# Queueing the query transposition and the copy of the sinks' keys behind the softmax reciprocal

## Chip, core and metric

The kernel runs on one core of a Trainium2 chip. The metric is the device time of one execution in microseconds (us). Three runs of the kernel before took 1175.45, 1173.58 and 1175.04 us; their median is 1175.04 us.

## What is computed

Three stages follow one another. Attention works on 4 batches of 8 heads, 768 positions and 64 channels; each position sees the first `n_sink` = 4 keys and a window of 128 keys. A dense layer with a piecewise activation follows, and then a layer of 8 experts in which each expert takes the 384 tokens that the greedy order of the gate's logits gives it.

```python
scores = scale * np.matmul(q, k.transpose(0, 1, 3, 2))
keep = is_sink | in_window
scores = np.where(keep, scores, -1000000000.0)
scores = scores - np.max(scores, axis=-1, keepdims=True)
a = np.exp(scores)
a = a / (np.sum(a, axis=-1, keepdims=True) + 1e-09)
x = np.matmul(a, v)                      # then (tokens, 512)
h = x @ w_in
g = np.where(h >= 1, h, np.where(h <= -1, 0.0, (h + 1) ** 2 / 4.0))
x = g @ w_out
for e in range(8):                       # tokens by the gate's logits, 384 each
    out[mask] = np.maximum(x[mask] @ w1[e], 0.0) @ w2[e]
```

## The kernel before

The 3072 tokens are cut into 12 blocks of 256, three per batch. Every product of the main path is made of three float32r products of high and low halves, so most tiles come in two parts (`xh` and `xl`, `gh` and `gl`, `sq` and `ql`).

**Attention** of a block runs over four pairs of heads (`attn_steps`; the first two blocks use `attn_steps_f32`, which the change does not touch). In a pair, `load_kq` fetches keys and queries, already cut into blocks of 32, so that one VectorE instruction in `turned` (line 428) transposes them in place. `trans_k` splits the transposed keys into `ks` (ScalarE line 300, VectorE line 301) and copies the 32 sinks' keys beside them (line 306). `trans_q` transposes the queries (line 428 on the tile `qr`) and splits them into `sq` (ScalarE, line 314) and `ql` (VectorE, line 315). `scores` has two matmuls (lines 332 and 333), a VectorE instruction that adds the mask and takes the maximum (335), and the exponential on ScalarE with the sum (337). `norm` of a head adds 1e-9 (342), takes the reciprocal of the two sums (343) and has GpSimd scale the 576 probabilities `pr` of a row in place (351; in the first block of a batch two instructions, 346 and 348). `ptrans` transposes the scaled probabilities on TensorE (370) and splits them into `pt` (372, 373). `pv` multiplies by the values and adds the halves to `xa` (389, 395, 396), and `split` turns `xa` into the layer's input: GpSimd adds (405 or 408), ScalarE makes `xh` (409), GpSimd makes `xl` (410). `split_v` has GpSimd write the values' low half (287).

**The dense layer** (`moe1_steps`) goes over 16 slices of the hidden width per block: `hid` has 12 matmuls (632), two VectorE and two ScalarE instructions (640 to 643), and GpSimd writes `gl` (644); `proj` of the slice two back has 12 matmuls (657). The dense layer of one block runs beside the attention of a later one, and TensorE takes both in one queue.

**The order.** `pipeline` (line 598) strings the steps of the pairs together: while pair `now` goes through `ptrans` and `pv`, the next pair's scores and norms are issued, and then `trans_k` and `trans_q` of the pair two on:

```python
"ptrans0 ptrans1 strans +s00 +s01 +norm0 pv0 +s10 +s11 +norm1 "
"*trans_k *trans_q ^load_kq pv1 +split_v +sinks *load_v split"
```

`Plan` sorts all steps by planned times. A scheduler then puts each engine's instructions into a queue; it may move an instruction ahead of an earlier traced one wherever data allows it. On the chip each engine takes its queue in order. The tiles `ks`, `sq` and `ql` have one buffer each. After the last block's attention the router picks the tokens and the experts run.

Of the kernel before, what the change touches and what calls it, by code (L numbers as in the profile page):

```python
# [1 line left out]

# [5 lines left out]
F32 = mybir.dt.float32  # L8
# [17 lines left out]
P = 128  # L26
NT = S // P
NS = 32
# [46 lines left out]
class Kernel:  # L75
# [174 lines left out]
    def attn_steps(self, blk, xt):  # L250

        nc, a = self.nc, self.a
# [4 lines left out]
        nk = len(kts)  # L257
        for p in range(H // 2):
            st = {}
# [36 lines left out]
            def trans_k(p=p, st=st):  # L296
                ks = st["ks"] = self.at.tile([P, 2, 3, W], F32R, name="ks", tag="ks")
                ps = self.turned(st["k"][:, :4 * nk].rearrange("p n c -> p (n c)")).rearrange("p (t c) -> p t c", c=P)
                for hh, (hs, os) in enumerate(half):
                    nc.scalar.copy(ks[hs, hh, :nk, :P], ps[hs])  # L300
                    nc.vector.tensor_tensor(out=ks[os, hh, :nk, :P], in0=ps[hs], in1=ks[hs, hh, :nk, :P].bitcast(F32),  # L301
                                            op=OP.subtract)
                if first:
                    self.sk[p] = self.kp.tile([P, 2, NS], F32R, name="sk", tag=f"sk{p}")
                    nc.vector.tensor_copy(self.sk[p], ks[:, :, 0, :NS].bitcast(F32))
                nc.vector.tensor_copy(ks[:, :, :nk - 1, P:],
                                      self.sk[p].bitcast(F32).unsqueeze(2).to_broadcast([P, 2, nk - 1, NS]))

            def trans_q(st=st):
                sq = st["sq"] = self.at.tile([P, 2, 2, P], F32R, name="sq", tag="sq")  # L310
                ql = st["ql"] = self.at.tile([P, 2, 2, P], F32R, name="ql", tag="ql")
                x = self.turned(st["q"].rearrange("p h n c -> p (h n c)"))
                flat = lambda t: t.rearrange("p h u q -> p (h u q)")
                nc.scalar.activation(flat(sq), x, AF.Copy, scale=0.125)
                nc.vector.scalar_tensor_tensor(flat(ql), x, 0.125, flat(sq).bitcast(F32), op0=OP.mult, op1=OP.subtract)
# [24 lines left out]
            def norm(hh, st=st):  # L340
                pr, sm = st["pr"][:, :, :, hh], st["sm", hh]
                nc.vector.tensor_scalar(sm[:, 2], sm[:, 1], 1e-9, None, op0=OP.add)
                nc.vector.reciprocal(sm[:, 2], sm[:, 2])  # L343
                r = sm[:, 2]
                if first:
                    nc.gpsimd.tensor_tensor(out=pr[:, 0, W:], in0=pr[:, 0, W:], in1=r[:, 0:1].to_broadcast([P, P]),
                                            op=OP.mult)
                    nc.gpsimd.tensor_tensor(out=pr[:, 1], in0=pr[:, 1], in1=r[:, 1:2].to_broadcast([P, 2 * P + NS]),
                                            op=OP.mult)
                else:  # L350
                    nc.gpsimd.tensor_tensor(out=pr, in0=pr, in1=r.unsqueeze(2).to_broadcast([P, 2, 2 * P + NS]),  # L351
                                            op=OP.mult)
# [67 lines left out]
    def load_blocks(self, t, src, ts):  # L420

        for j in range(2):
            blocks = src[ts[0] * P:(ts[-1] + 1) * P, 32 * j:32 * j + 32].rearrange("(n s) d -> s n d", s=32)
            self.nc.sync.dma_start(t[32 * j:32 * j + 32, :4 * len(ts)], blocks)  # L424

    def turned(self, x):

# [947 lines left out]
@with_exitstack  # L1375
def tile_sink_window_attention__moe__expert_choice(ctx, tc, q, k, v, n_sink, window, w_in, w_out, wg, w1, w2, out):
    a = dict(q=q, k=k, v=v, n_sink=n_sink, window=window, w_in=w_in, w_out=w_out, wg=wg, w1=w1, w2=w2, out=out)
    nc = tc.nc
    K = Kernel(ctx, tc, a)
    K.c = ctx.enter_context(tc.tile_pool(name="const", bufs=1))  # L1380
    dr = ctx.enter_context(tc.tile_pool(name="dr", bufs=1, space=DRAM))
    K.x2d = dr.tile([N, DM], F32, name="x2d")
    xg = dr.tile([B * H * S, D], F32, name="xg")
    K.logits = K.c.tile([P, B * NT, E], F32, name="logits")
    K.sk, K.sv, K.skf, K.svf = {}, {}, {}, {}

    def pipeline(general):
        with ExitStack() as c0:
            c1, c3, c4, cd = (c0.enter_context(ExitStack()) for _ in range(4))
            K.pools(c1.enter_context, c0.enter_context)  # L1390
            K.front_pools(c3.enter_context)
            K.dec = cd.enter_context(tc.tile_pool(name="dec", bufs=2, side="right"))
            if not general:
                K.consts()
            xs = {}
            gw, w_in, w_out, gate_t, gate_m = K.weight_steps()

            def xtiles(b):
                if b not in xs:
                    xs[b] = tuple(K.xp.tile([P, 4, TB], F32R, name=n, tag=n) for n in ("xh", "xl"))  # L1400
                return xs[b]

            def attn(plan, blks, t0, t1):
                if general:
                    for i, b in enumerate(blks):
                        plan.at(t0 + (t1 - t0) * i / len(blks), lambda b=b: K.load_x(b, xg, *xtiles(b)))
                    return
                steps = K.pipeline([p for b in blks for p in (K.attn_steps_f32 if b < NF else K.attn_steps)(b, xtiles)])
                dt = 1 / (len(steps) - 0.5)
                for i, s in enumerate(steps):  # L1410
                    plan.add(t0 + (t1 - t0) * dt * (i - 0.5 * (i > 0)), t0 + (t1 - t0) * dt * (i + 0.5), s)

            K.turn_, K.free = 0, ["U0", "A", "U1", "R", "U2", "A"]
            plan = Plan(tc)
            attn(plan, range(1), 0, T0A)
            attn(plan, range(1, 2), A1, B1)
            plan.at(T0M, lambda: setattr(K, "free", ["A", "A", "R"]))
            x01 = [xtiles(1), xtiles(0)]
            plan.add(T0M, T00, K.moe1_steps(0, lambda: xtiles(0), part=(0, H0)))
            plan.add(T1, T2, K.moe1_steps(1, lambda: xtiles(1)))  # L1420
            plan.add(T2, T3, K.moe1_steps(0, lambda: xtiles(0), part=(H0, FT)))
            plan.at(1, gw)
            if not general:
                plan.at(T0A, K.flags)

            def late():
                cd.close()
                K.late_weights(c1.enter_context)

            for f in range(FT):  # L1430
                t, TD = (D0 + f * DA, DA) if f < H1 else (D1 + (f - H1) * DD, DD)
                plan.at(t if f < H1 else D1 + (f - H1) * DD * WF, lambda f=f: w_in(f))
                if f == FA:
                    plan.at(t + TD / 2, late)
                plan.at(t + TD / 2, lambda f=f: w_out(f))
                plan.at(t + TD / 2 + TG, lambda f=f: gate_t(f))
                plan.at(t + TD / 2 + TG + (TH if f < FA - 1 else 1), lambda f=f: gate_m(f))

            def turn():
                c3.close()  # L1440
                K.router_pools(c0.enter_context)
                hold.append(c4.enter_context(tc.tile_pool(name="hold", bufs=1, side="right")))
                K.router_consts()
                K.rtag = "R"

            def clear():
                c4.close()
                c1.close()
                K.pools2(c0.enter_context)

            hold = []
            b1 = T3 + BLOCK * (NB - 3)
            attn(plan, range(2, 3), TA2, TA3)
            attn(plan, range(3, NB), TA3, b1 - BLOCK * AHEAD)
            for b in range(2, NB - 1):
                plan.add(T3 + BLOCK * (b - 2 - OV), T3 + BLOCK * (b - 1), K.moe1_steps(b, lambda b=b: xtiles(b)))
            plan.at(b1 - BLOCK * OV - 0.5, turn)
            to_logits, rest = K.moe1_steps(NB - 1, lambda: xtiles(NB - 1), lambda: hold[0])
            plan.add(b1 - BLOCK * OV, b1 + HB, to_logits)
            plan.add(b1 + HB, b1 + HB + TP, rest)  # L1460
            plan.at(b1 + HB + TP, clear)
            K.experts(plan, b1 + HB)
            plan.run()

    pipeline(False)
    flag = nc.values_load(K.flag[0:1, 0:1], min_val=0, max_val=1)
    with tc.If(flag):
        with ExitStack() as c0:
            K.attn_general(c0.enter_context, xg)
        pipeline(True)  # L1470
# [32 lines left out]
```

## Time and profile before

| | |
|---|---|
| median of three runs | 1175.04 us |
| time of the profiled execution | 1172.83 us |
| its span (first to last instruction) | 1171.0 us |
| TensorE busy | 1102.2 us, 94% of the span |
| VectorE busy | 872.2 us, 74% |
| ScalarE busy | 698.2 us, 60% |
| GpSimd busy | 487.0 us, 42% |

The profile counts an engine as busy while an instruction of it runs. TensorE is the fullest. Its busy time is modelled from pipelined matmuls, so the rows that matter are those that give the idle time in front of an instruction and the instruction that ended it. In those rows PE is TensorE's matmul, DVE VectorE, ACT ScalarE and POOL GpSimd.

### The profile page before, as it was taken

Reading aid. Unit: us, or ns where it says so; the run is one execution under the profiler, and the core shown is the slowest. Engines: PE = TensorE matmul, PEld = TensorE weight load, DVE = VectorE, ACT = ScalarE, POOL = GpSimd, SP = SyncE. Lnnn points to the kernel's source line nnn. Section 1 sums busy time; section 2 is a strip of 40 time slices with the busy share of each in tenths; the row PEclk is TensorE's granted clock in tenths of the full one; section 3 lists DMA queues with packets and bytes.
Section 4 is the critical chain, followed back from the end, with each engine's and each line's share of the span. In section 5 each row is a group of like instructions: output and inputs, shape, how many; then the busy total and the mean of one; then the engine's idle time right before and its main releaser. Section 6 shows DMA issues by size and latency. Waiting matters only on the chain.

```text
span 1171.0 us, 24367 instructions
## 1 busy us (share of the span) xinstructions
PE 1102.2 (94%) x8256; PEld 1017.4 (87%) x8256; DVE 872.2 (74%) x2718; ACT 698.2 (60%) x1598; POOL 487.0 (42%) x590
## 2 busy tenths in 40 slices
PE   5899888999999999999999999999799999999997
PEld 3688878999999999999999999999587788788896
DVE  5978978777777877776777787755788888788430
ACT  4887777566666666676667676643245445444552
POOL 1335745444545545455545554542213213322321
PEclk9899999999999999999999999999799999999999
DMA  4645522323222222223222222100485767667772
GB/s 105 173 143 158 158 60 61 70 42 64 53 39 56 36 55 49 61 46 64 34 54 49 58 46 56 22 19 1 120 228 168 204 180 216 188 194 202 217 218 66
DMA packets 241928, 118.13 MB, mean 101 GB/s; under 512 B 196096, under 2 KB 220672, under 8 KB 241792
## 3 DMA queue, kind: packets, MB, share of 16 engines
q1 hardware_dynamic: 231504, 85.36, 28.4%
q0 software_dynamic: 8592, 29.89, 10.9%
q8 instruction: 67, 1.10, 0.4%
q10 hardware_dynamic: 1696, 1.22, 0.3%
q14 instruction: 69, 0.57, 0.2%
HBM read 86.00 MB, written 13.11 MB: 85 GB/s over the span
## 4 chain that ended last, share of the span: by engine, by line
PE 42%; DVE 13%; issue 9%; ACT 6%; POOL 5%; DMA 4%; SPq 2%; DVEq 0%; POOLq 0%; ACTq 0%
PE hp L632 11%; PE up L657 11%; PE hp L1048 6%; PE us L1075 6%; PE xp L389 1%; DVE oh L945 1%; ACT pr L337 1%; ACT u L641 1%; PE tp L370 1%; SPq L424 1%; DVE u L640 1%; DVE ind L801 1%; DVE ks L301 1%; DMA qr<-in_q_dram 1%; POOL gl L644 1%
## 5 line engine op out<-in xcount | busy, mean ns | idle before, releaser
L644 POOL TENSOR_TENSOR gl<-u,gh 128x256 fp32r<-128x256 f32 x192 | 149.5, 779 | 205.3 <-ACT gh L643 169.5
L657 PE MATMUL up<-woh,gl 128*128 128x256 f32 x576 | 166.6, 289 | 2.6 <-POOL gl L644 2.6
L657 PE MATMUL up<-woh,gh 128*128 128x256 f32 x576 | 163.7, 284 | 0.0
L657 PE MATMUL up<-wol,gh 128*128 128x256 f32 x576 | 163.5, 284 | 0.0
L641 ACT ACTIVATE u<-u,half 128x256 f32<-128x256 f32 x192 | 97.4, 508 | 83.4 <-DVE u L640 79.4
L632 PE MATMUL hp<-xh,wil 128*128 128x256 f32 x768 | 132.0, 291 | 3.6 <-ACT xh L409 2.8
L632 PE MATMUL hp<-xl,wih 128*128 128x256 f32 x768 | 126.4, 284 | 2.0 <-POOL xl L410 1.6
L632 PE MATMUL hp<-xh,wih 128*128 128x256 f32 x768 | 124.7, 283 | 0.0
L632 PEld LDWEIGHTS hp<-xh,wil 128*128 128x128 f32 x768 | 107.6, 191 | 5.7 <-ACT xh L409 4.2
L657 PEld LDWEIGHTS up<-woh,gl 128*128 128x128 f32 x576 | 108.9, 189 | 3.2 <-POOL gl L644 3.1
L632 PEld LDWEIGHTS hp<-xl,wih 128*128 128x128 f32 x768 | 106.4, 191 | 3.4 <-POOL xl L410 3.4
L657 PEld LDWEIGHTS up<-wol,gh 128*128 128x128 f32 x576 | 108.6, 189 | 0.4 <-issue 0.4
L657 PEld LDWEIGHTS up<-woh,gh 128*128 128x128 f32 x576 | 108.5, 188 | 0.4 <-issue 0.4
L632 PEld LDWEIGHTS hp<-xh,wih 128*128 128x128 f32 x768 | 106.3, 191 | 0.0
L642 DVE TENSOR_TENSOR u<-hp,u 128x256 f32<-128x256 f32 x192 | 80.5, 420 | 31.6 <-ACT u L641 29.8
L640 DVE TENSOR_SCALAR u<-hp 128x256 f32<-128x256 f32 x192 | 79.9, 416 | 31.0 <-PE hp L632 22.5
L351 POOL TENSOR_TENSOR pr<-pr,sm 128x576 f32<-128x576 f32 x56 | 71.3, 1273 | 67.9 <-DVE sm L343 30.3
L643 ACT CAST gh<-u 128x256 fp32r<-128x256 f32 x192 | 77.6, 404 | 30.3 <-DVE u L642 28.0
L337 ACT ACTIVATE pr<-pr,sm 128x288 f32<-128x288 f32 (+1 forms) x160 | 85.2, 533 | 16.3 <-DVE sm L335 15.7
L1056 ACT ACTIVATE hh<-hp 128x384 fp32r<-128x384 f32 x64 | 31.5, 492 | 102.1 <-PE hp L1048 89.4
L373 DVE TENSOR_TENSOR pt<-tp,pt 128x512 fp32r<-128x512 f32 (+1 forms) x80 | 51.3, 647 | 43.9 <-ACT pt L372 43.4
L1075 PE MATMUL us<-w2h,hl 128*128 128x512 f32 x192 | 80.8, 421 | 0.0
(264 smaller groups left out, 3040.0 us busy)
## 6 DMA issues: line engine op xcount, KB each, us to landing
w1r<-in_moe_w_dram SPq DMA_DIRECT2D x32, 512.0 KB, 4.7
w2r<-in_moe_w_dram SPq DMA_DIRECT2D x32, 512.0 KB, 4.5
w2l<-w2r POOLq DMA_DIRECT2D x32, 512.0 KB
qr<-in_q_dram SPq DMA_DIRECT2D x320, 32.0 KB, 1.9
dr<-in_moe_w_in_dram SPq DMA_DIRECT2D x15, 512.0 KB, 4.1
dr<-in_moe_w_out_dram SPq DMA_DIRECT2D x15, 512.0 KB, 3.7
x2d<-ev SPq DMA_DIRECT2D x26, 256.0 KB, 2.2
vr<-in_v_dram SPq DMA_DIRECT2D x56, 96.0 KB, 2.3
```

Source lines behind the costliest of these rows:

```text
L337: nc.scalar.activation(pr, pr, AF.Exp, bias=sm[:, 0, u:u + 1], scale=-1.0, accum_out=sm[:, 1, u:u + 1])
L351: nc.gpsimd.tensor_tensor(out=pr, in0=pr, in1=r.unsqueeze(2).to_broadcast([P, 2, 2 * P + NS]), op=OP.mult)
L373: nc.vector.tensor_tensor(out=pt[:, 1, :n], in0=ps, in1=pt[:, 0, :n].bitcast(F32), op=OP.subtract)
L632: nc.tensor.matmul(ps, w_[:, k, fs], x_[:, k, :], start=(i == 0 and k == 0), stop=(i == 2 and k == 3))
L640: nc.vector.tensor_scalar(u, ps, -1.0, 1.0, op0=OP.max, op1=OP.min)
L641: nc.scalar.activation(u, u, AF.Square, bias=self.half, scale=0.5)
L642: nc.vector.tensor_tensor(out=u, in0=ps, in1=u, op=OP.max)
L643: nc.scalar.copy(gh, u)
L644: nc.gpsimd.tensor_tensor(out=gl, in0=u, in1=gh.bitcast(F32), op=OP.subtract)
L657: nc.tensor.matmul(o, g_[:, ts], self.w_out_part(w_, f)[:, cs], start=(f == fa and i == 0 and (cs.start > 0 or t == 0)), stop=(f == fz - 1 ...
L1048: nc.tensor.matmul(ps, w_[:, k, fs], x_[:, k, :], start=(i == 0 and k == 0), stop=(i == 2 and k == 3))
L1075: nc.tensor.matmul(us[j], h_[:, o], w_[:, f % 2, :], start=(f == 0 and i == 0), stop=(f == nf - 1 and i == 2))
```

## The change

Two VectorE instructions of the preparation of a pair, the sinks' copy (line 306) and the transposition of the queries (line 428 on `qr`), get an ordering edge without a semaphore: the scheduler may not put them ahead of the reciprocal that was traced last. No instruction is added or removed. The transposition of the keys, the split of the keys (line 301) and `ql` carry no edge. The first attention block that goes through `attn_steps` has no reciprocal to stand behind for its first pair; the other 39 pairs do.

```diff
-                nc.vector.tensor_copy(ks[:, :, :nk - 1, P:],
-                                      self.sk[p].bitcast(F32).unsqueeze(2).to_broadcast([P, 2, nk - 1, NS]))
+                with self.behind_shares():
+                    nc.vector.tensor_copy(ks[:, :, :nk - 1, P:],
+                                          self.sk[p].bitcast(F32).unsqueeze(2).to_broadcast([P, 2, nk - 1, NS]))
...
-                x = self.turned(st["q"].rearrange("p h n c -> p (h n c)"))
+                with self.behind_shares():
+                    x = self.turned(st["q"].rearrange("p h n c -> p (h n c)"))
...
-                nc.vector.reciprocal(sm[:, 2], sm[:, 2])
+                self.shares = nc.vector.reciprocal(sm[:, 2], sm[:, 2]).ins
...
+    def behind_shares(self):
+
+        return self.tc.issue_after(self.shares) if self.shares else nullcontext()
```

`issue_after(i)` gives every instruction traced in its block on the engine of `i` such an edge to `i`. In `norm` of the second head, whose reciprocal is the last one ahead of `trans_k` and `trans_q`, this is what the queues hold. The changed file's lines stand 1 to 6 lower: 306 is 307, 428 is 434, 342 and 343 are 344 and 345, 315 is 317, 396 is 398, 640 and 642 are 646 and 648, 351 is 353, 644 is 650, 405 and 408 are 407 and 410, 410 is 412.

Blocks are counted from 0 and named by the pair whose second norm it is. VectorE, third pair of block 7, before (`sm` are the sums, `ks` the keys, `qr` the queries):

```order
L642 TENSOR_TENSOR u<-hp,u 128x256
L306 CAST ks<-sk 128x2x2x32
L342 TENSOR_SCALAR sm<-sm 128x2
L428 STREAM_TRANSPOSE qr<-qr 128x512
L343 RECIPROCAL sm<-sm 128x2
L301 TENSOR_TENSOR ks<-kr,ks 64x3x128
L396 TENSOR_TENSOR xa<-xp,xa 64x512
L315 SCALAR_TENSOR_TENSOR ql<-qr,sq 128x512
```

and in the changed kernel:

```order
L648 TENSOR_TENSOR u<-hp,u 128x256
L344 TENSOR_SCALAR sm<-sm 128x2
L345 RECIPROCAL sm<-sm 128x2
L307 CAST ks<-sk 128x2x2x32
L434 STREAM_TRANSPOSE qr<-qr 128x512
L301 TENSOR_TENSOR ks<-kr,ks 64x3x128
L398 TENSOR_TENSOR xa<-xp,xa 64x512
L317 SCALAR_TENSOR_TENSOR ql<-qr,sq 128x512
```

The copy and the transposition have moved from ahead of the reciprocal to just behind it; `ql` keeps its place. GpSimd's queue at the same place before (`pr` are the probabilities that wait for the reciprocal):

```order
L351 TENSOR_TENSOR pr<-pr,sm 128x576
L644 TENSOR_TENSOR gl<-u,gh 128x256 x2
L351 TENSOR_TENSOR pr<-pr,sm 128x576
L408 TENSOR_TENSOR xa<-xa 128x2x128
```

and in the changed kernel:

```order
L353 TENSOR_TENSOR pr<-pr,sm 128x576
L650 TENSOR_TENSOR gl<-u,gh 128x256
L353 TENSOR_TENSOR pr<-pr,sm 128x576
L650 TENSOR_TENSOR gl<-u,gh 128x256
L410 TENSOR_TENSOR xa<-xa 128x2x128
```

The second scaling has passed one `gl`. A second shape, VectorE at the first pair of block 8, before:

```order
L342 TENSOR_SCALAR sm<-sm 128x2
L315 SCALAR_TENSOR_TENSOR ql<-qr,sq 128x512
L642 TENSOR_TENSOR u<-hp,u 128x256
L343 RECIPROCAL sm<-sm 128x2
L396 TENSOR_TENSOR xa<-xp,xa 64x512
```

and in the changed kernel:

```order
L344 TENSOR_SCALAR sm<-sm 128x2
L345 RECIPROCAL sm<-sm 128x2
L307 CAST ks<-sk 128x2x2x32
L434 STREAM_TRANSPOSE qr<-qr 128x512
L648 TENSOR_TENSOR u<-hp,u 128x256
L398 TENSOR_TENSOR xa<-xp,xa 64x512
L317 SCALAR_TENSOR_TENSOR ql<-qr,sq 128x512
```

Since the transposition now stands behind the reciprocal, `ql`, which reads it, does too. A third place, GpSimd at the first pair of block 7, where `xa` and `xl` of block 6's last pair are made, before:

```order
L351 TENSOR_TENSOR pr<-pr,sm 128x576
L405 TENSOR_TENSOR xa<-xa 128x128
L644 TENSOR_TENSOR gl<-u,gh 128x256
L287 TENSOR_TENSOR v_6769<-vr,v_6769 128x6x64
L410 TENSOR_TENSOR xl<-xa,xh 128x256
```

and in the changed kernel:

```order
L353 TENSOR_TENSOR pr<-pr,sm 128x576
L407 TENSOR_TENSOR xa<-xa 128x128
L412 TENSOR_TENSOR xl<-xa,xh 128x256
L650 TENSOR_TENSOR gl<-u,gh 128x256
L287 TENSOR_TENSOR v_6769<-vr,v_6769 128x6x64
```

Here `xl` has passed one `gl` and the values' low half. TensorE's queue differs in block 2 and at three places behind it, the last at the first pair of block 3 (224 us in the trace), and nowhere later; the queue of SyncE, which issues the loads, is the same.

## Rows read from the trace of the kernel before

**Rows 1.** Busy us of engines by stretch (instructions), TensorE's granted clock, DMA share, GB/s.

```profile
core 0: us, PE busy (x) PEld busy (x) DVE busy (x) ACT busy (x) POOL busy (x), PEclk, DMA share, GB/s
205.00:770.00 565.00, 545.39 (x4456) 539.31 (x4455) 428.18 (x1197) 376.39 (x959) 285.21 (x355) 0.99 0.25 49
```

**Rows 2.** Waits of TensorE's matmuls: us in total, times, longest us.

```profile
PE tp L370 <- POOL pr L351: 15.1, 15, 2.0
...
PE hp L632 <- ACT xh L409: 2.8, 5, 1.5
...
PE hp L632 <- POOL xl L410: 1.6, 2, 1.2
PE tp L370 <- POOL pr L346: 1.0, 1, 1.0
```

**Rows 3.** Timeline, third pair of block 7: start, us, instruction [idle before, releaser].

```profile
495.78 0.22 DVE L306 CAST ks<-sk 128x128 fp32r<-128x128 f32 x1
495.91 0.16 DVE L342 TENSOR_SCALAR sm<-sm 128x2 f32<-128x2 f32 x1
496.19 0.71 DVE L428 STREAM_TRANSPOSE qr<-qr 128x512 f32<-128x512 f32 x1
496.82 0.12 DVE L343 RECIPROCAL sm<-sm 128x2 f32<-128x2 f32 x1
496.88 0.73 POOL L644 TENSOR_TENSOR gl<-u,gh 128x256 fp32r<-128x256 f32 x1 [3.11 <-issue]
497.56 1.47 POOL L351 TENSOR_TENSOR pr<-pr,sm 128x576 f32<-128x576 f32 x1
499.08 0.75 PE L370 MATMUL tp<-ident,pr 128*128 128x128 f32 x4 [1.92 <-POOL pr L351]
```

**Rows 4.** Timeline of TensorE: first and last of the five such waits.

```profile
313.59 0.74 PE L370 MATMUL tp<-ident,pr 128*128 128x128 f32 x4 [0.88 <-POOL pr L351]
...
747.51 0.75 PE L370 MATMUL tp<-ident,pr 128*128 128x128 f32 x4 [1.07 <-POOL pr L351]
```

**Rows 5.** Timeline, first pair of block 8, where ql stands ahead of the reciprocal.

```profile
526.53 0.68 DVE L315 SCALAR_TENSOR_TENSOR ql<-qr,sq 128x512 fp32r<-128x512 f32 x1
527.47 0.15 DVE L343 RECIPROCAL sm<-sm 128x2 f32<-128x2 f32 x1
528.97 0.75 PE L370 MATMUL tp<-ident,pr 128*128 128x128 f32 x4 [1.25 <-POOL pr L351]
```

**Rows 6.** Timeline, first pair of block 10.

```profile
647.86 0.90 DVE L342 TENSOR_SCALAR sm<-sm 128x2 f32<-128x2 f32 x1
649.30 0.12 DVE L343 RECIPROCAL sm<-sm 128x2 f32<-128x2 f32 x1
650.71 0.85 PE L370 MATMUL tp<-ident,pr 128*128 128x128 f32 x4 [1.99 <-POOL pr L351]
```

**Rows 7.** Timeline, third pair of block 5: VectorE between the sums and the reciprocal.

```profile
376.04 0.56 DVE L301 TENSOR_TENSOR ks<-kr,ks 64x384 fp32r<-64x384 f32 x1
```

**Rows 8.** Timeline, first pair of block 7: GpSimd, and TensorE's wait for xl.

```profile
466.04 0.72 POOL L644 TENSOR_TENSOR gl<-u,gh 128x256 fp32r<-128x256 f32 x1
466.72 1.01 POOL L287 TENSOR_TENSOR v<-vr,v 128x384 fp32r<-128x384 f32 x1
468.47 0.39 PE L632 MATMUL hp<-xl,wih 128*128 128x256 f32 x1 [1.16 <-POOL xl L410]
```

**Rows 9.** As rows 1: two stretches behind long waits.

```profile
347.00:351.00 4.00, 4.00 (x22) 3.94 (x23) 1.96 (x7) 1.54 (x5) 0.00 (x0) 0.57 0.16 26
651.00:655.00 4.00, 4.00 (x23) 4.00 (x23) 1.49 (x3) 1.78 (x4) 1.95 (x3) 0.57 0.30 48
```

**Rows 10.** Timeline: ql and the next scores, for block 7 and for block 6.

```profile
498.76 0.81 DVE L315 SCALAR_TENSOR_TENSOR ql<-qr,sq 128x512 fp32r<-128x512 f32 x1
502.74 0.29 PE L332 MATMUL sc<-ks,ql 128*128 128x288 f32 x1
436.90 1.27 DVE L315 SCALAR_TENSOR_TENSOR ql<-qr,sq 128x512 fp32r<-128x512 f32 x1
438.80 0.33 PE L332 MATMUL sc<-ks,ql 128*128 128x128 f32 x1
```

More of the change, by code (lines that the diff above doesn't have):

```diff
@@ L1 @@
-from contextlib import ExitStack
+from contextlib import ExitStack, nullcontext
 import concourse.bass as bass
@@ L1385, in tile_sink_window_attention__moe__expert_choice @@
     K.sk, K.sv, K.skf, K.svf = {}, {}, {}, {}
+    K.shares = None
     def pipeline(general):
+        K.shares = None
         with ExitStack() as c0:
```

## Prediction

> **What bounds the kernel now.** I read the windows by stage first, then TensorE's waits, then the timeline in front of each wait. From 205 to 770 us, while the dense layer and attention share TensorE, it is busy 545.4 of 565 us; VectorE is busy 428 and GpSimd 285 us [rows 1]. So TensorE sets the pace, no other engine is full, and only what lets TensorE stand idle can be won: 19.6 us there. The table of waits says what ends that idle time. The largest entry is the transposition of the probabilities (line 370) waiting for GpSimd's scaling (line 351): 15.1 us in 15 waits, with 1.0 us more where line 346 scales. Next come the dense layer's matmuls waiting for `xh` and `xl` at the turn of a block, 2.8 and 1.6 us [rows 2].
>
> The timeline shows what is late behind such a wait [rows 3]. The add of 1e-9 starts at 495.91; the reciprocal needs nothing but that, yet starts at 496.82, since VectorE first takes the 0.71 us transposition of the queries. The copy of the sinks' keys (0.22 us) stood just ahead as well. Then GpSimd, in queue order, does a `gl` (0.73 us) before the scaling, which runs from 497.56 to 499.03, and TensorE, idle for 1.92 us, goes on at 499.08. The reader should see two delays in series, both of them queue order and not data.
>
> **The change, term by term.** It removes and adds no work; it moves two VectorE instructions behind the reciprocal, and the scheduler answers on GpSimd and ScalarE. I count idle time in front of TensorE's instructions, from the profiled execution (1172.83 us).
>
> *Five waits of the shape just read* (the first and last of them 0.88 and 1.07 us, together 6.33 us) [rows 3, 4]. The reciprocal starts 0.91 us behind the start of the add; whatever comes next on VectorE starts 0.28 behind it, as the transposition did, so the reciprocal moves by 0.63; the copy gives up to 0.13 more; the scaling passes a `gl`, 0.73. That makes 1.4 to 1.5 us, more than four of the five waits. The fifth, 1.92, keeps 0.45. Gain 5.9 us. The `gl` that is passed comes up to 1.5 us later. Its matmuls are those of the slice two back in TensorE's queue, so 24 matmuls and more lie between, and I charge nothing; without that cover it would cost up to 1.47 us a time, 7 us in all.
>
> *Two waits where `ql` stands ahead of the reciprocal* (1.25 us, and another like it of 1.16 at 714.6) [rows 5]. `ql` costs 0.68 us and lies between sums and reciprocal; behind it a dense-layer instruction goes too. I take 0.8 each: 1.6 us. The 1.0 us wait for line 346 has `ql` and a `gl` ahead of it and goes whole: 1.0.
>
> *The wait of 1.99 us* [rows 6] and one of 0.46 of its shape. The transposition accounts for 0.62. The add itself took 0.90 us instead of the 0.16 of [rows 3], while GpSimd wrote a values' low half; in the new order the low half stands behind the scaling. The 0.74 between the two is an upper bound, nothing the lower; I take 1.3 and 0.46: 1.8 us.
>
> *One wait in block 5* has only the keys' split (0.56 us) between sums and reciprocal, which now goes behind [rows 7]: 0.6 us. The waits before 205 us, where weights are still decoded and TensorE's own order changes, I set at 0, with 3 us either way.
>
> *The turns of blocks.* `xl` waited behind a `gl` of 0.72 and a low half of 1.01 us at 468.47 [rows 8]; both now stand behind it. Where block 4 ends, `xa` passes a `gl` in the same way. Of the 4.4 us for `xh` and `xl` [rows 2] I take 3.0, with 0 and 4.4 as ends.
>
> *The clock.* Behind two of the long waits the granted clock is down: its mean over 4 us is 0.57 and 0.57 [rows 9], where 0.5 is 1.2 GHz and 1 is 2.4. So 43% of 4 us, 1.7 us, is lost each time. One follows the wait of 1.99 us, the other one for `xh` of 1.5. Waits that shrink may leave the clock at 2.4 GHz; I count one of the two, 1.7, with 0 and 3.4 as ends.
>
> *What becomes late.* The transposition leads to `sq` on ScalarE, to `ql`, and to the next pair's scores. In block 7 `ql` ends 3.17 us before TensorE takes those scores, in block 6 only 0.63 [rows 10]. In most pairs `ql` keeps its place behind the keys' split and `xa`, so nothing moves. In the blocks that open a batch the margin is under 1.5 us in five pairs, and there the transposition now comes directly ahead of `ql`; I charge 1.5 us in all, with 0 and 5 × 0.71 = 3.6 as ends. One more us goes to waits that TensorE meets because it arrives earlier.
>
> Sum: 5.9 + 1.6 + 1.0 + 1.8 + 0.6 + 3.0 + 1.7 − 1.5 − 1.0 = 13.1 us. The execution becomes 1159.7; the median of the runs stood 2.2 above the execution, so the median becomes **1161.9 us**.
>
> **A rule against it.** VectorE's add of two columns grew from 0.16 to 0.90 us beside a GpSimd instruction [rows 3, 6]. The Trainium skill, page "SBUF — State Buffer", section "Who interferes with whom", says that the two engines share one port pair, held for a whole instruction, and that copies and tensor-scalar operations can need it; this row agrees. By that rule the change is dangerous: the sinks' copy now stands exactly where GpSimd starts to scale, and if GpSimd gets there first, the copy and the transposition behind it wait for the whole scaling. That is the third rival.
>
> **Rivals.**
> 1. *Half of it is given back.* TensorE, released earlier, waits for the next thing instead (`pt`, `gl`, `xh`). For it: ScalarE takes `sq` ahead of `pt` in its queue. Against: the margin of 3.17 us. Only half of the 10.9 us of scaling waits is kept: 1167.4. Chance 0.15.
> 2. *All of it comes, and the clock with it.* All 16.1 us of line 370, 4.4 of the turns and 3.4 of clock: 1175.0 − 23.9 = 1151.1. Against: waits that are longer than the delay removed. Chance 0.14.
> 3. *The copy is locked out.* The transposition and `ql` come later by one scaling, up to 1.47 us. The typical margin covers it; five pairs of small margin pay about 1.15 each: 1161.9 + 5.8 = 1167.7. Chance 0.08.
> 4. *The reciprocal's place decides nothing.* If the scaling is released by something that the profile does not name, the waits stay: 1175.0. Against: VectorE is named in the timeline. Chance 0.07.
> 5. *Slower: ScalarE stands at `sq`.* In many pairs the transposition was done well before the reciprocal, so that `sq` found it ready; now it ends up to 0.12 + 0.22 + 0.71 = 1.05 us behind. ScalarE takes its queue in order, and `pt`, `xh` and the values stand behind `sq`. If TensorE lost 0.7 us in each of 35 pairs, that is 24.5 us against 13.1: 1161.9 + 24.5 = 1186.4. It decides from 0.4 us a pair. Against: ScalarE is idle a third of the time, and TensorE does not wait for `pt` now. Chance 0.06.
>
> **How the numbers follow.** The forecast has 0.50. A change of under 0.2% (2.3 us) is about what a measurement of this kernel cannot tell from none. Faster are the forecast and rivals 1 to 3: 0.87; the same is rival 4: 0.07; slower is rival 5: 0.06. The range leaves out rivals 4 and 5 and a part of rival 2. From the bounds, the forecast alone spans 1155 to 1168; with the rivals kept it is 1152 to 1172.
>
> **What would show it.** Right: the entry of line 370 waiting for line 351's scaling falls from 15.1 us to 3 to 6; the reciprocal follows its add within 0.3 us at all 39 places; `xh` and `xl` together fall under 2 us; TensorE's idle time from 205 us to the end of the dense layer falls by 10 or more. Rivals 1, 3 and 5 would show as new rows: matmuls of scores waiting for `ql`, or ScalarE idle at `sq` and TensorE waiting for `pt` or `xh`. I am wrong if the entry of line 370 stays above 10 us, or if it falls and the span does not follow.

## Result and profile after

Four runs of the changed kernel took 1157.49 to 1159.9 us, median **1158.62 us**; four of the kernel before, beside them, had a median of 1174.4. The ratio is 0.9868, with a 95% interval from 0.9857 to 0.988: faster by 1.3%. The profiled execution took 1158.95 us (span 1157.2) against 1172.83 (1171.0): 13.9 us less, where the prediction's sum had 13.1.

The windows by stage of the changed kernel, with the columns of [rows 1]:

```profile
205.00:770.00 565.00, 556.63 (x4588) 551.53 (x4587) 438.46 (x1242) 384.80 (x977) 292.40 (x374) 1.00 0.26 51
347.00:351.00 4.00, 4.00 (x35) 4.00 (x35) 3.13 (x12) 2.46 (x8) 0.74 (x1) 1.00 0.64 190
```

TensorE is busy 556.6 of 565 us, against 545.4 in [rows 1]: 11.2 us of its idle time are gone. In the second stretch the clock is 1.00, where [rows 9] had 0.57. TensorE's waits after the change; each row, called an entry below, gives the us in total, the times and the longest:

```profile
PE sc L334 <- DVE ql L317: 3.4, 6, 1.9
PE hp L638 <- ACT xh L411: 3.2, 4, 1.4
PE sc L334 <- DVE pt L375: 2.3, 5, 1.0
PE tp L372 <- POOL pr L353: 2.0, 6, 0.5
PE hp L638 <- POOL xl L412: 1.1, 4, 0.5
PE xp L391 <- DVE st L365: 1.0, 1, 1.0
```

Against [rows 2], the wait for scaled probabilities fell from 15.1 to 2.0 and the wait for line 346's scaling is gone. `xh` and `xl` together went from 4.4 to 4.3 only. Scores now wait for `ql` (3.4, 1.7 before) and for `pt` (2.3), and one product waits for `st`. The place of [rows 3] in the changed kernel's timeline, VectorE and GpSimd in order of time, then TensorE:

```profile
490.78 0.17 DVE L344 TENSOR_SCALAR sm<-sm 128x2 f32<-128x2 f32 x1
490.98 0.17 DVE L345 RECIPROCAL sm<-sm 128x2 f32<-128x2 f32 x1
491.06 0.20 DVE L307 CAST ks<-sk 128x128 fp32r<-128x128 f32 x1
491.29 1.17 POOL L353 TENSOR_TENSOR pr<-pr,sm 128x576 f32<-128x576 f32 x1 [2.56 <-ACT ks L300]
491.36 0.71 DVE L434 STREAM_TRANSPOSE qr<-qr 128x512 f32<-128x512 f32 x1
492.41 1.06 POOL L650 TENSOR_TENSOR gl<-u,gh 128x256 fp32r<-128x256 f32 x1
492.51 0.74 PE L372 MATMUL tp<-ident,pr 128*128 128x128 f32 x4
```

The reciprocal starts 0.20 us behind its add and the scaling 0.51 behind it; in [rows 3] these were 0.91 and 1.65. TensorE does not wait here at all.

### The profile page after: what moved, and what is told of

It is laid out like the page before. It is cut to its first block, busy times and chain, and to the rows that moved or that the text cites. A ratio compares the mean times of both kernels' runs of the same rounds, so it can differ in the third digit from the quotient of the medians.

```text
span 1157.2 us, 24364 instructions
## 1 busy us (share of the span) xinstructions
PE 1099.3 (95%) x8256; PEld 1014.8 (88%) x8256; DVE 873.0 (75%) x2718; ACT 698.7 (60%) x1598; POOL 485.6 (42%) x590
## 4 chain that ended last, share of the span: by engine, by line
PE 58%; DVE 19%; issue 8%; ACT 5%; DMA 4%; POOL 4%; SPq 1%; ACTq 0%; POOLq 0%; DVEq 0%
PE hp L638 17%; PE up L663 16%; PE hp L1054 6%; PE us L1081 6%; PE xp L391 2%; DVE ks L301 2%; PE tp L372 2%; PE sc L334 1%; DVE df L244 1%; PE sc L335 1%; DVE oh L951 1%; DVE u L646 1%; DVE df L242 1%; DVE ind L807 1%; DVE df L239 1%
## 5 line engine op out<-in xcount | busy, mean ns | idle before, releaser
L650 POOL TENSOR_TENSOR gl<-u,gh 128x256 fp32r<-128x256 f32 x192 | 152.8, 796 | 188.1 <-ACT gh L649 164.0
L353 POOL TENSOR_TENSOR pr<-pr,sm 128x576 f32<-128x576 f32 x56 | 65.5, 1169 | 68.3 <-DVE ks L307 31.5
L1081 PE MATMUL us<-w2h,hh 128*128 128x512 f32 x192 | 75.6, 394 | 0.0
```

What stands on the lines that cost most here:

```text
L650: nc.gpsimd.tensor_tensor(out=gl, in0=u, in1=gh.bitcast(F32), op=OP.subtract)
L1081: nc.tensor.matmul(us[j], h_[:, o], w_[:, f % 2, :], start=(f == 0 and i == 0), stop=(f == nf - 1 and i == 2))
```

## Experiments

Theory A: the transposition delayed the reciprocal on VectorE. Its rivals: B, the copy did; C, GpSimd's `gl` ahead of the scaling did. In e5 TensorE's queue is that of the changed kernel, in e8 that of the kernel before; in e1 and in e4 it differs from the changed kernel's at one place each, before 200 us.

### e1 and e2: one edge at a time

```diff
-                with self.behind_shares():
-                    nc.vector.tensor_copy(ks[:, :, :nk - 1, P:], ...)
+                nc.vector.tensor_copy(ks[:, :, :nk - 1, P:], ...)
```

> Only the transposition of the queries is queued behind the reciprocal; the sinks' copy stands free again, ahead of the reciprocal of most pairs. Theory A (the transposition's 0.7 us ahead of the reciprocal, and the order of gl that follows from it on GpSimd, made the waits): nearly the whole gain, 1159 to 1160.5 us against 1158.6 for the full change and 1174.4 before; the entry of the TensorE waits for scaled probabilities stays at 2 to 4 us. Rival B (the copy of 0.2 us decides): 1168 us or more, that entry at 8 us or more.

> Only the sinks' copy is queued behind the reciprocal; the transposition stands free. Theory A: 1172.5 to 1175 us, the entry of waits for scaled probabilities at 12 to 16 us (15.1 before), GpSimd's gl still ahead of the second scaling. Rival B: 1160 to 1166 us with that entry at 6 us or less. If both edges count about alike, this and e1 both come out near 1166.

The diff is e1's; e2 takes the edge off the transposition in the same way. e1: 1162.88 us, ratio 0.9902 [0.9886, 0.9919]. e2: 1174.75, ratio 1.0009 [0.9998, 1.0021]. The entries for scaled probabilities, e1 and then e2:

```profile
PE tp L371 <- POOL pr L352: 3.3, 8, 0.7
```

```profile
PE tp L371 <- POOL pr L352: 12.2, 16, 1.7
```

B falls: the copy's edge alone buys no time, as the transposition then still stands ahead of the reciprocal. (Its entry did fall by 2.9 us, and the time did not follow.) But e1 missed its band by 2.4 us: with the transposition out of the way, the copy's place is worth some 4 us. In e1's trace 1.3 us of them are the entry above, 1.0 is `xl` (2.1), and the granted clock has a mean of 0.58 from 345 to 349 us, behind a wait for `xh` of 1.77 us (1.37 in the changed kernel, with the clock at 1.00). The account is not closed: from 170 to 174 us e1's clock is at 1.00 where the changed kernel's has a mean of 0.57. Nor does e1 tell A from C, for GpSimd takes as many `gl` ahead of each scaling in e1 as in the changed kernel. That is left to e5 and e8.

### e5: the gl back in front, VectorE as changed

```diff
+                    with self.tc.issue_after(self.gl) if p == 2 and hh and blk >= 4 else nullcontext():
-                    nc.gpsimd.tensor_tensor(out=pr, in0=pr, ...)
+                        nc.gpsimd.tensor_tensor(out=pr, in0=pr, ...)
...
+            self.gl = nc.gpsimd.tensor_tensor(out=gl, in0=u, in1=gh.bitcast(F32), op=OP.subtract).ins
```

> From the changed kernel: in the third pair of a block the scaling is queued behind the gl that it had passed, so GpSimd's order is that of the kernel before at the five waits of one shape, and one place more (block 5); the queues of the other engines are those of the changed kernel, instruction for instruction. Theory C (the gl of 0.73 us ahead of the scaling was half of these waits): with 0.6 to 0.7 us won on VectorE alone, the waits of 0.88, 1.92, 1.51, 0.95 and 1.07 us come back as about 0.2, 1.2, 0.8, 0.3 and 0.4, 2.9 us together: 1160.5 to 1162 us, the entry of waits for scaled probabilities at 4.5 to 5.5 us (2.0 in the changed kernel). Rival (the reciprocal's place alone freed them, there is slack behind it): 1158.3 to 1159.3 us with that entry at 2 to 2.5 us.

1166.98 us, ratio 0.995 [0.9935, 0.9965]. Its profiled execution has a span of 1163.2 us, 6.0 above the changed kernel's, and six waits account for it: 1.08, 1.48, 1.05, 0.88 and 0.86 us at the five places, and 0.86 in block 5, where neither kernel had a `gl` in front; 6.2 together. That is twice what I expected. The place of [rows 3] in e5:

```profile
492.09 0.17 DVE L344 TENSOR_SCALAR sm<-sm 128x2 f32<-128x2 f32 x1
492.29 0.17 DVE L345 RECIPROCAL sm<-sm 128x2 f32<-128x2 f32 x1
492.62 0.41 ACT L650 CAST gh<-u 128x256 fp32r<-128x256 f32 x1
493.15 0.74 POOL L651 TENSOR_TENSOR gl<-u,gh 128x256 fp32r<-128x256 f32 x1 [3.10 <-issue]
493.85 1.47 POOL L354 TENSOR_TENSOR pr<-pr,sm 128x576 f32<-128x576 f32 x1
495.37 0.39 PE L373 MATMUL tp<-ident,pr 128*128 128x128 f32 x1 [1.48 <-POOL pr L354]
```

The reciprocal is as early as in the changed kernel, and it helps little. GpSimd holds its place for a `gl` whose input `gh` ScalarE ends only at 493.03; the scaling starts 1.76 us behind the add, no sooner than the 1.65 before. What e5 still wins at these places comes from the add itself: here it starts 2.42 us behind the start of TensorE's last matmul of these scores, against 2.98 before, and at four of the five places it is earlier by 0.15 to 0.57.

### e8: GpSimd as changed, VectorE as before

```diff
-            nc.gpsimd.tensor_tensor(out=gl, in0=u, in1=gh.bitcast(F32), op=OP.subtract)
+            self.low.append((gl, lambda: nc.gpsimd.tensor_tensor(out=gl, in0=u, in1=gh.bitcast(F32), op=OP.subtract)))
...
+                    if p == 2 and hh and blk >= 4:
+                        self.keep = False
+                        with self.tc.issue_after(i.ins):
+                            self.lows()
```

`lows` issues the `gl` that were put off (elsewhere at once, here behind the scaling `i`). Beside the five places a few instructions move by a place or two: on GpSimd at three places (452, 530 and 629 us in the trace before), on VectorE and ScalarE mostly where a batch opens.

> From the kernel before, without the edges: in the third pair of a block the gl is issued behind the scaling, as the changed kernel has it at the five waits of one shape; VectorE keeps the transposition ahead of the reciprocal there (a few splits of sinks and of keys move by a place where a batch opens). The mirror image of e5. If the two delays run side by side (the scaling starts behind the later of reciprocal and gl, as e5 shows: 1.48 us were left of 1.92 with VectorE's part alone), GpSimd's place alone gives 0.5 to 0.8 us at each of five places: 1169.5 to 1172 us against 1174, entry of waits for scaled probabilities at 11.5 to 13 us. If GpSimd's place is all of it, the five waits go whole, 6.3 us: 1166 to 1168.5 us, entry at 9 us. If it gives nothing without the reciprocal: 1173.5 to 1175 us.

1167.06 us, ratio 0.9938 [0.9926, 0.9951]. The time lies in the band of "GpSimd's place is all of it", the rows do not: the entry for scaled probabilities is 12.4 us, and the five waits are 0.36, 1.43, 0.99, 0.42 and 0.58 us, each some 0.5 shorter, none gone. The place of [rows 3] in e8, and a wait for `xh`:

```profile
494.79 0.12 DVE L344 RECIPROCAL sm<-sm 128x2 f32<-128x2 f32 x1
495.06 1.45 POOL L352 TENSOR_TENSOR pr<-pr,sm 128x576 f32<-128x576 f32 x1 [3.32 <-DVE sm L344]
496.57 0.74 PE L375 MATMUL tp<-ident,pr 128*128 128x128 f32 x4 [1.43 <-POOL pr L352]
...
345.92 0.39 PE L644 MATMUL hp<-xh,wil 128*128 128x256 f32 x1 [1.66 <-ACT xh L414]
```

Now the reciprocal, behind the transposition, holds the scaling: 1.18 us behind the add. So the two delays ran **side by side**, and the scaling starts behind the later one; neither A nor C is the whole cause. VectorE's part alone (e5) took 6.33 − 5.35 = 1.0 us off the five waits, GpSimd's alone (e8) 6.33 − 3.78 = 2.55, both together all 6.33. Most of the rest of e8's gain (its span is 6.4 us shorter) is the clock: the half-clock stretches of [rows 9] are gone from this trace, 3.4 us. Line 348's waits, 0.7 us, are gone as well.

### e6: behind the mask in place of the reciprocal

```diff
+                mask = nc.vector.tensor_tensor_reduce(out=pr, in0=ps[:, o], in1=m, ...)
+                if u:
+                    self.shares = mask.ins
...
-                self.shares = nc.vector.reciprocal(sm[:, 2], sm[:, 2]).ins
+                nc.vector.reciprocal(sm[:, 2], sm[:, 2])
```

> The same two edges, but behind the last mask-and-maximum of the pair's scores in place of the reciprocal: the copy and the transposition no longer delay the mask, but mostly stand between mask and reciprocal. Theory A (the reciprocal is what was late): most of the gain is gone, 1167 to 1174 us, with 10 us or more of waits for scaled probabilities. Rival M (it was the mask, and with it ScalarE's exponentials, that the transposition made late; the 0.7 us fit beside the exponential): 1159 to 1163 us.

1177.21 us, ratio 1.0035 [1.0022, 1.0048]. Rival M falls, and A's band was too good: this is slower than the kernel before. The entry for scaled probabilities is 17.0 us. The scheduler, which sees the reciprocal later still, also puts a `gl` ahead of the second scaling in ten more pairs than before.

### e4: the remainders too

```diff
+                    with self.behind_shares():
-                    nc.vector.tensor_tensor(out=ks[os, hh, :nk, :P], in0=ps[hs], ...)
+                        nc.vector.tensor_tensor(out=ks[os, hh, :nk, :P], in0=ps[hs], ...)
...
+                with self.behind_shares():
-                nc.vector.scalar_tensor_tensor(flat(ql), x, 0.125, ...)
+                    nc.vector.scalar_tensor_tensor(flat(ql), x, 0.125, ...)
```

> The two remainders are queued behind the reciprocal too: the keys' remainder (0.3 us each, two a pair) and ql. Theory A goes on (whatever stands ahead of the reciprocal costs its own length where TensorE waits): the 2.0 us that are left of the waits for scaled probabilities fall to about 1, but ql is later by one or two operations, so that the scores' wait for ql grows from 3.4 us to 4 to 6: 1158.5 to 1161 us. Rival (the remainders ahead of the reciprocal still cost, and ql has slack): 1156 to 1157.5 us.

1189.61 us, ratio 1.0128 [1.0109, 1.0147]: far outside both bands, 31 us above the changed kernel. The edge on `ql` moves no instruction of any queue (`ql` reads the transposition, which has the edge already), so all of it is the keys' remainder. The wait for probabilities falls as expected, to 1.4 us, but the turn of a block takes its place:

```profile
PE hp L640 <- ACT xh L413: 14.4, 8, 2.6
```

The turn from block 5 to block 6 in e4:

```profile
411.73 0.70 DVE L436 STREAM_TRANSPOSE qr<-qr 128x512 f32<-128x512 f32 x1
412.28 0.74 POOL L652 TENSOR_TENSOR gl<-u,gh 128x256 fp32r<-128x256 f32 x1 [1.31 <-issue]
412.35 0.72 DVE L308 CAST ks<-sk 128x64 fp32r<-128x64 f32 x1
413.10 0.69 DVE L400 TENSOR_TENSOR xa<-xp,xa 64x512 f32<-64x512 f32 x1
413.87 1.23 POOL L412 TENSOR_TENSOR xa<-xa 128x256 f32<-128x256 f32 x1 [0.85 <-DVE xa L400]
415.58 0.39 PE L640 MATMUL hp<-xh,wil 128*128 128x256 f32 x1 [2.60 <-ACT xh L413]
```

VectorE's add for `xa`, on which all four pairs' input to the next block hangs, stands behind the whole preparation that was pushed back. Moving work behind the reciprocal moves it in front of `xa`. That is why the remainders have to stay free. Longer waits for `xh` are 11.2 of the 31 us. Half clock at three of them (near 350, 476 and 606 us, where the changed kernel has none) is some 6.8 more, and the scores' waits for `ql` and `pt` grew by 4.3; the rest is not broken down.

### e3, e9 and e10: the edges from block 3 on

```diff
-                self.shares = nc.vector.reciprocal(sm[:, 2], sm[:, 2]).ins
+                share = nc.vector.reciprocal(sm[:, 2], sm[:, 2]).ins
+                self.shares = share if blk >= 3 else None
```

> The edges hold from the block of index 3 on; the first blocks that are computed so keep the order of before. Theory: the 1.4 to 2.1 us by which the changed kernel's transposes of the probabilities stood behind those of before at 167 to 207 us came from the late ql and transposition of these blocks, and come back whole: 1156.6 to 1157.6 us. Rival: they are met by a wait that follows (as the shift of -0.48 at 285 us may say), so that nothing is left of them at the end: 1158 to 1159.5 us.

> The changed kernel once more, unedited, beside e10 and e11 on one chip, to see whether a difference of 0.2% is one: 1157.5 to 1160 us, 3 us above e10.

> The kernel of e3 once more, unedited, beside e9: 1154.5 to 1157 us. Theory (the early blocks lose 2.8 us by the edges): 2.2 to 3.5 us under e9. Rival (a difference of chips or of the first 160 us): within 1.2 us of e9.

e3: 1155.83 us, ratio 0.9845 [0.9827, 0.9864], 0.8 under its band; e10, the same kernel on another chip, is 1.7 above it, so the gain is read on one chip. There e9 (the changed kernel) took 1159.68 us, 1158.88 to 1160.9, and e10 1157.54, 1156.67 to 1158.06: 2.1 us less, with ranges that do not touch. The gap is a little under the band of 2.2 to 3.5. In the traces e10's transposes of the probabilities run 0.1 us ahead of e9's at 165 us and 2.8 at 284 us. So the loss in the first blocks was real, and most of it was not met by a later wait. Scores of block 2, first in the changed kernel, then in e10:

```profile
185.14 0.37 PE L334 MATMUL sc<-ks,ql 128*128 128x288 f32 x1 [1.86 <-DVE ql L317]
```

```profile
185.38 0.37 PE L334 MATMUL sc<-ks,ql 128*128 128x288 f32 x1 [1.29 <-DVE ql L317]
```

The wait of 0.98 us for `st`, at 211.27 in the changed kernel, is absent from e10. **The kernel of e3 beats both.**

### e7 and e11: the turn of a block

Both start from e3. e7 queues the next pair's low half behind GpSimd's add at a turn (and traces `split` ahead of `split_v`); e11 queues the transposition of a block's last pair behind VectorE's add (and traces `trans_q` behind `pv1` there).

```diff
+                with self.tc.issue_after(self.xlast) if self.xlast else nullcontext():
-                nc.gpsimd.tensor_tensor(out=v2[:, :nk, :, 1, :], in0=vr, ...)
+                    nc.gpsimd.tensor_tensor(out=v2[:, :nk, :, 1, :], in0=vr, ...)
...
-                nc.vector.tensor_tensor(out=xa, in0=ps[0:64], in1=xa, op=OP.add)
+                add = nc.vector.tensor_tensor(out=xa, in0=ps[0:64], in1=xa, op=OP.add)
+                if p == 3 and hh and blk >= 3:
+                    self.shares = add.ins
```

> From e3 (1155.83 us): where a block ends, the low half of the next pair's values is queued on GpSimd behind the add that makes xa, so that xa, xh and xl of the turn no longer stand behind it (1.0 us at 338.77 us of e3, where xa starts 0.4 us after VectorE's part is there). Theory T (what is left of the turns' waits, 2.7 us for xh and 1.6 for xl, is made by GpSimd's queue): 1153.5 to 1155.2 us, xh and xl together at 2.5 us or less. Rival: the values come late instead and TensorE waits for them, or the turn is set by VectorE's own add: 1155.5 us or more.

> From e3: in the last pair of a block the transposition is queued behind VectorE's add of xa, which the turn of the block waits for. Theory V (the transposition of 0.7 us ahead of xa keeps the turns' waits up): xh and xl together fall from 4.3 to 3 us or less, 1153 to 1155.3 us. Rival (xa is bound by ScalarE's copy and by GpSimd, or ql comes late at the next scores): 1155.5 to 1158 us.

e7: 1159.21 us, ratio 0.9876 [0.9861, 0.989]. That is 1.7 us above e10, and `xh` and `xl` are 2.8 and 2.5 us: the edit misses the band of Theory T, but it does not test T. Its turn into block 5, VectorE's add, GpSimd and then TensorE:

```profile
339.29 0.68 DVE L400 TENSOR_TENSOR xa<-xp,xa 64x512 f32<-64x512 f32 x1
340.04 1.25 POOL L653 TENSOR_TENSOR gl<-u,gh 128x256 fp32r<-128x256 f32 x1 [0.70 <-POOL pr L355]
341.25 0.72 POOL L412 TENSOR_TENSOR xa<-xa 128x256 f32<-128x256 f32 x1
341.93 1.00 POOL L288 TENSOR_TENSOR v<-vr,v 128x384 fp32r<-128x384 f32 x1
342.89 0.73 POOL L415 TENSOR_TENSOR xl<-xa,xh 128x256 fp32r<-128x256 f32 x1
...
342.46 0.39 PE L641 MATMUL hp<-xh,wil 128*128 128x256 f32 x1 [1.07 <-ACT xh L414]
```

The low half has left its place ahead of `xa`, and a `gl` of 1.25 us has taken it; the low half now stands ahead of `xl`. GpSimd's `xa` still starts 1.28 us behind the end of VectorE's add, held by GpSimd's own queue, so what T says was neither removed nor refuted. e11: 1156.14 us (1155.29 to 1157.98), ratio 0.9845 [0.983, 0.986], beside 1157.54 of e10. Its ranges overlap e10's, its median lies in the rival's band, and its `xh` and `xl` are 2.8 and 1.1 us where e10 has 2.7 and 1.5. A gain of under 1.5 us is possible and not shown.

## Why the prediction was right, and where it was not

The direction, the size and the place were right: TensorE's idle time behind the scaling went, and the time followed. The median came 3.3 us under the 1161.9 of the forecast: 0.8 is the sum, and the other 2.5 the offset of 2.2 between median and profiled execution, which was added on and which the changed kernel does not have (its median stands 0.3 under). Of the signs, the entry fell further than said (2.0), and TensorE's idle time fell by more than 10 us; but `xh` and `xl` did not fall under 2 us, and at ten of 40 pairs the reciprocal still starts 0.4 to 1.4 us behind its add. Term by term, from the two profiled executions:

| term | predicted | measured |
|---|---|---|
| five waits of one shape | 5.9 | 6.33, all gone |
| two waits with `ql` ahead | 1.6 | 2.41, both gone |
| line 346's wait | 1.0 | 1.0, gone |
| 1.99 and 0.46 | 1.8 | 2.16; 0.29 left of the first |
| block 5 | 0.6 | 1.51, gone |
| turns of blocks | 3.0 | 0.1 |
| clock | 1.7 | 3.4 |
| later `ql`, waits met earlier | −2.5 | −5.0 |

The last row is 1.7 more for `ql`, 2.3 for `pt` and 1.0 for `st`. The measured column sums to 11.9; 0.7 of line 348's waits and 0.7 of smaller ones before 205 us bring it to 13.3, and the spans differ by 13.8. The agreement with the predicted 13.1 is luck in part: the errors of several terms cancel.

**The five waits.** The size held and the structure failed. The prediction read "two delays in series" in [rows 3] and gave the reciprocal 0.63 and the passed `gl` 0.73. e5 and e8 show them side by side, and the trace before shows it already: the `gl` starts at 496.88, ahead of the reciprocal's end at 496.94, and 0.13 us behind the end of its input `gh` on ScalarE.

```profile
496.34 0.41 ACT L643 CAST gh<-u 128x256 fp32r<-128x256 f32 x1
```

So that `gl` stood behind `gh`, and an earlier reciprocal would not have made it earlier. Whoever had moved only VectorE's two instructions with GpSimd's queue held as it was would have won 1.0 us of 6.33. That the edges on VectorE also moved GpSimd's order is what made them pay, and only the order of the queues tells that. One gain the prediction did not count: with both delays gone the scaling runs beside the transposition and not beside the keys' remainder, and takes 1.17 us in place of 1.47.

**The waits of [rows 5, 6].** In these first pairs GpSimd has as many `gl` ahead of the scaling as before, and the waits of 1.25 and 1.16 us went whole and 1.70 of the 1.99, where the prediction took only part (0.8 of each, 1.3 of 1.99). For [rows 5] that leaves VectorE's order as the cause; at [rows 6] a values' low half moved as well. No run undid these places by themselves, but the others agree: e5 has the waits of the changed kernel there, e8 has 1.30, 1.70 and 1.18 us, e1 0.45, 0.73 and 0.37, and e2 0.83, 0.70 and 0.83. So both edges count at these places, and GpSimd's order in third pairs does not.

**Block 5** [rows 7]. I counted the keys' split between sums and reciprocal, 0.56 us, and 1.51 went. Missed was the other end of the chain: the transposition also stood ahead of the last mask. VectorE there, before and then after the change:

```profile
373.03 0.70 DVE L428 STREAM_TRANSPOSE qr<-qr 128x512 f32<-128x512 f32 x1
373.66 0.38 DVE L640 TENSOR_SCALAR u<-hp 128x256 f32<-128x256 f32 x1
373.97 0.43 DVE L335 CUSTOM_DVE_ANT_0 pr<-sc,m 128x288 f32<-128x288 f32 x1
```

```profile
370.30 0.42 DVE L646 TENSOR_SCALAR u<-hp 128x256 f32<-128x256 f32 x1 [0.58 <-PE hp L638]
370.64 0.45 DVE L337 CUSTOM_DVE_ANT_0 pr<-sc,m 128x288 f32<-128x288 f32 x1
```

In the kernel before, `u` and the mask follow the transposition without a pause; after, VectorE is idle ahead of them. The mask's delay, 0.66 us against its scores, goes into the exponential and the sums. The scaling there took 1.59 us, too, and takes 1.16 now. How the 1.51 divides among these no run shows.

**The turns** failed as a term. In [rows 8] `xl` did stand behind a `gl` and a low half, and that wait of 1.16 us is gone. But other turns have waits of the same size. The turn into block 5, before the change and then after it (the 1.53 and 1.37 us are the waits for `xh`):

```profile
344.13 0.73 POOL L644 TENSOR_TENSOR gl<-u,gh 128x256 fp32r<-128x256 f32 x1
344.82 0.72 POOL L408 TENSOR_TENSOR xa<-xa 128x256 f32<-128x256 f32 x1
...
346.03 0.39 PE L632 MATMUL hp<-xh,wil 128*128 128x256 f32 x1 [1.53 <-ACT xh L409]
```

```profile
341.49 0.69 DVE L398 TENSOR_TENSOR xa<-xp,xa 64x512 f32<-64x512 f32 x1
341.60 1.02 POOL L287 TENSOR_TENSOR v<-vr,v 128x384 fp32r<-128x384 f32 x1
342.57 1.18 POOL L410 TENSOR_TENSOR xa<-xa 128x256 f32<-128x256 f32 x1
...
342.20 0.96 DVE L317 SCALAR_TENSOR_TENSOR ql<-qr,sq 128x512 fp32r<-128x512 f32 x1
...
344.24 0.39 PE L638 MATMUL hp<-xh,wil 128*128 128x256 f32 x1 [1.37 <-ACT xh L411]
```

`xa` did pass the `gl` of 0.73. But `ql` now runs beside it, and `xa` takes 1.18 us in place of 0.72: 0.46 of the 0.73 is given back. The values' low half also still stands ahead of it: VectorE's add is done at 342.17, and GpSimd's `xa` starts at 342.57.

**Before 205 us**, set at 0 with 3 either way, the change lost 1.4 us by 207 us (the transposes of the probabilities stand that much later), and 2.8 by 284 us against the kernel without early edges (e9 against e10). The 1.4 lie inside the bound.

**Rival 1**, half given back, came in part: 5.0 us went into new waits. **Rival 2**, all of it and the clock, came in large part: 14.1 of the 16.1 us of scaling waits and the 3.4 of the clock, but only 0.1 of the turns' 4.4. **Rival 3**, the copy locked out: at the place shown above the copy starts 0.23 us ahead of the scaling and takes 0.20, and the transposition beside the scaling takes its 0.71. In the stretch from 205 to 790 us one copy took 0.65 us, with a median of 0.205 (last section). In e4 the copy does take longer, with a median of 0.649. **Rivals 4 and 5** fall by the result. e4 is rival 5's neighbour: a preparation pushed too far does cost more than the change wins, but through `xa`, not through `sq`.

## What to carry to other kernels

When a wait ends behind two instructions on two engines, ask whether they run in series or side by side; the gain of either alone tells, and it may be next to nothing. An order edge on one engine makes a scheduler re-sort the others: read every queue before costing it. And what is queued behind one urgent instruction lands in front of the next, so push back only what has slack, and not in the stretch where the queue has none.

## Hardware behaviour that was not expected

**The clock does not follow the length of a wait alone.** Before the change, 1.53 us of waiting for `xh` are followed by four microseconds at a mean of 0.57 [rows 9], where 0.5 is 1.2 GHz. In e8 the wait at the same point of the program is 1.66 us, and the clock stays at 1.00, 2.4 GHz:

```profile
347.00:351.00 4.00, 4.00 (x35) 4.00 (x35) 2.84 (x10) 1.84 (x5) 0.74 (x1) 1.00 0.35 102
```

The 12 runs of e2 show that the clock varies within one kernel: five with a mean granted clock of 0.984 or 0.985 took 1172.47 to 1174.33 us, seven with 0.978 to 0.982 took 1174.75 to 1177.73. Between kernels it is no mere chance: the mean is 0.978 to 0.982 in all runs of the kernel before that stand beside e1 to e11, and 0.984 or 0.985 in all eight of the changed kernel. So the price of a wait in clock cannot be read from its length; what decides it no run here shows. The Trainium skill, page "TensorE: Matmul & The Clock Gate", section "What's actually happening", says of a kernel's start that the number of slow matmuls varies between runs of one kernel. e2's runs show a spread too; at which place of the kernel, a mean does not tell.

**GpSimd and VectorE slow each other by kind of instruction.** The scaling takes 1.47 us beside the keys' remainder [rows 3] and in e5, and 1.17 beside the transposition. The remainder in [rows 3]:

```profile
496.98 1.04 DVE L301 TENSOR_TENSOR ks<-kr,ks 64x384 fp32r<-64x384 f32 x1
```

It takes 0.56 in [rows 7], where GpSimd is idle. The sinks' copy, between 205 and 790 us, in the changed kernel and then in e4 (ns: least, median, most):

```profile
L307 DVE CAST ks<-sk x36: 172/205/650, 206.8 to 731.1; 128x128 fp32r<-128x128 f32 x24, 128x64 fp32r<-128x64 f32 x12
```

```profile
L308 DVE CAST ks<-sk x36: 195/649/926, 208.2 to 764.0; 128x128 fp32r<-128x128 f32 x24, 128x64 fp32r<-128x64 f32 x12
```

In e4's rows above, the copy starts 0.07 us behind a `gl` and ends 0.05 behind it. The Trainium skill, page "SBUF — State Buffer", section "Who interferes with whom", says that whichever of the two takes the shared ports first holds them for a whole instruction, that copies can need them, and that a VectorE instruction with one input from SBUF, outside the modes that use both pairs of ports, does without. The copy in e4 agrees with the first two; the transposition, 0.71 us beside the scaling and alone, with the last.
